# Both feed-forward products by one level of Strassen's algorithm, with the activations in DRAM

## The chip, the cores and the metric

The kernel runs on one core of a Trainium2 chip. A core has five engines that run side by side and meet only at semaphores: TensorE (matrix products, in the profile PE, with its weight loads as PEld), VectorE (DVE), ScalarE (ACT), GpSimd (POOL) and SyncE (SP), which here only issues DMAs. TensorE writes to PSUM, a small memory of eight banks of 128 x 512 float32; everything else works in SBUF. The metric is the device time of one execution in microseconds, lower is better, as the median of several runs.

## The reference

Four batches of eight heads of 768 tokens with 64 features each go through an attention in which a query sees only the keys of its own hash bucket, and then through a gated feed-forward block. Float64 weights come in, float32 goes out.

```python
q_bucket, k_bucket = 6-bit hashes of q @ proj > 0, k @ proj > 0     # proj is 64 x 6
mask = q_bucket[:, :, :, None] == k_bucket[:, :, None, :]
scores = where(mask, q @ k.T / 8, -1e9)
x = softmax(scores) @ v                     # (4, 8, 768, 64) -> 3072 tokens x 512
h = x @ w_in                                # 512 x 2048
g = h * (1.0 / (1.0 + exp(-1.702 * h)))
out = g @ w_out                             # 2048 x 512 -> 3072 x 512
```

## The kernel before

**Attention** (`attention`, from L198) works on 16 pairs: two heads of one batch at a time, side by side on the 128 partitions. A pair is cut into groups `(n, c, kt)`: a half `c` of its queries and two blocks of 128 keys, six groups a pair. For each key block `scores` (L268) writes the products of keys and queries for both heads to a PSUM tile `ps`: first the float32 product of `kT` and `qT`, then, added to it in the same PSUM tile, a bf16 product of the bit features `kf` and `qf`, which is zero where the buckets match and very large and negative where they don't. ScalarE takes the exponential of it into `es` (L276). One group later `values` (L294) multiplies `es` with `v` into `av`, and `add` (L280) adds the key blocks up, two of three additions on GpSimd (L286) and the rest on VectorE (L289, L292). At the end of a half, `total` (L302) sums over the partitions with a matmul (`dn`), `invert` (L308) makes the reciprocal on VectorE, and `norm` (L319) writes the result into `xT`, which holds all 3072 tokens as the right-hand operand of the feed-forward. During pair n, pair n + 1 is loaded, turned and hashed (`turn`, `hashed`, `featured`), and one chunk of 128 x 512 of `w_in` is converted from float64 bits to float32 (`convert`, L122): four VectorE passes, a square on ScalarE (L140), an addition on GpSimd (L144), and a last VectorE pass (L147) that waits for it.

After the last group, L388 to L391 find the largest squared norm, by a reduction, a transpose on TensorE and another reduction. Should it be too large, a safe form of everything (`shifted_attention` and a second feed-forward) runs after L525; with these inputs it doesn't.

**Feed-forward** (`feed_forward`, L465) goes over six blocks of 512 tokens. `hidden` (L492) makes the 2048 rows of `g` for one block: 16 PSUM tiles `h`, each the sum of four matmuls of 128 x 128 weights with 512 tokens, each followed by the activation on ScalarE (L499). `outputs` (L502) makes the 512 tokens' results: four PSUM tiles `y`, each the sum of 16 matmuls with 128 x 128 of `g` as weights and 512 columns of `w_out`, copied by VectorE (L510) and stored (L512). `g` stays in SBUF. While `hidden(0)` and `hidden(1)` run, `w_out` is converted, one chunk of 128 x 512 for every two activations.

**Order.** TensorE, VectorE, ScalarE and GpSimd run their instructions in the order in which the program writes them; the DMA issues on SP are placed by the framework. A tile pool gives every name a number of buffers; a new tile waits until the one that had its buffer before has been read for the last time. Pools are freed at the end of their `with` or `ExitStack`, and what comes after waits for the last readers of that memory.

Of the kernel before, what the change touches and what calls it, by code (L numbers as in the profile page):

```python
# [19 lines left out]
P = 128  # L20
# [18 lines left out]
def kernel(  # L39
# [57 lines left out]
    for x, signs in (("q", (1.0, -1.0)), ("k", (-1.0, 1.0))):  # L97
# [4 lines left out]
        for j in range(2):  # L102
# [11 lines left out]
    w_out_sb = const.tile([P, FC, DM], F32, name="w_out_sb")  # L114
# [5 lines left out]
    CW = 512  # L120

    def convert(cv, dst, src):  # L122

        raw = cv.tile([P, CW, 2], U32, tag="raw", name="raw")
        nc.sync.dma_start(out=raw, in_=src)
        lo, hi = raw[:, :, 0], raw[:, :, 1]
# [12 lines left out]

        nc.scalar.activation(size, hi.bitcast(F32), Act.Square)  # L140
        yield
        nc.vector.scalar_tensor_tensor(dst, lo, 2.0**-52, sign.bitcast(F32), op0=Alu.mult, op1=Alu.mult)  # L142
        yield
        nc.gpsimd.tensor_tensor(dst, bits.bitcast(F32), dst, op=Alu.add)  # L144
        yield

        nc.vector.scalar_tensor_tensor(dst, size, (1.125 * 2.0**-15) ** 2, dst, op0=Alu.is_ge, op1=Alu.mult)  # L147
# [3 lines left out]
    in_chunks = [(w_in_sb[:, kc, f : f + CW], wi[kc, :, f : f + CW]) for f in range(0, FF, CW) for kc in range(KC)]  # L151
    out_chunks = [(w_out_sb[:, fc, d : d + CW], wo[fc, :, d : d + CW]) for fc in range(FC) for d in range(0, DM, CW)]


    def load(ld, n, v_bufs=2):
# [39 lines left out]
        return steps  # L195


    def attention():  # L198


        actx = ExitStack()
        with actx:
            ld = actx.enter_context(tc.tile_pool(name="ld", bufs=1))
            wk = actx.enter_context(tc.tile_pool(name="wk", bufs=2))
            ep = actx.enter_context(tc.tile_pool(name="ep", bufs=1))
            cv = actx.enter_context(tc.tile_pool(name="cv", bufs=1))
            st = actx.enter_context(tc.tile_pool(name="st", bufs=2))
            sps = actx.enter_context(tc.tile_pool(name="sps", bufs=2, space=PSUM))
            aps = actx.enter_context(tc.tile_pool(name="aps", bufs=2, space=PSUM))
            mps = actx.enter_context(tc.tile_pool(name="mps", bufs=2, space=PSUM))  # L210


            es = [ep.tile([P, T, 2, HS + 1], F32, name=f"e{i}") for i in range(2)]
# [43 lines left out]
                                     start=True, stop=True)  # L257

            def featured(n, name):
                f = wk.tile([P, HS], BF16, tag=f"{name}b", name=f"{name}b")  # L260
                nc.vector.tensor_scalar(f, dots.pop((n, name)), above[name][:, 0:1], FEAT[name], op0=Alu.is_gt, op1=Alu.mult)
                for j in range(2):
                    for c in range(2):
                        r0 = D * c + 32 * j
                        nc.sync.dma_start(out=feats[n % 2][name][D * j : D * j + 32, c * HS : (c + 1) * HS],  # L265
                                          in_=f[r0 : r0 + 32, :])

            def scores(n, c, kt):  # L268
                qT, kT, qf, kf = xts[n, "q"], xts[n, "k"], feats[n % 2]["q"], feats[n % 2]["k"]
                keys, cols = slice(kt * P, (kt + 1) * P), slice(c * HS, (c + 1) * HS)  # L270
                ps = sps.tile([P, 2, 512], F32, tag="s", name="ps")
                for a, m, last in ((kT, qT, False), (kf, qf, True)):
                    for j in range(2):
                        hs = slice(D * j, D * (j + 1))
                        nc.tensor.matmul(ps[:, j, 0:HS], a[hs, keys], m[hs, cols], start=not last, stop=last)  # L275
                nc.scalar.activation(es[c][:, kt, :, 0:HS], ps[:, :, 0:HS], Act.Exp, scale=1.0 / D**0.5)  # L276
# [31 lines left out]
            def invert(n, c):  # L308
# [7 lines left out]
                rd = accs[n, c] = st.tile([P, HS], F32, tag="rd", name="rd", bufs=1)  # L316
                nc.vector.transpose(rd.rearrange("p (s i) -> p s i", i=32), r.to_broadcast([P, HS // 32, 32]))  # L317

            def norm(n, c):  # L319
# [11 lines left out]

            def step():
                next(conv[0], None)


            fetch(0, "k")
# [8 lines left out]
            for g in range(len(groups) + 3):  # L345
# [27 lines left out]
                if n < last:  # L373
# [11 lines left out]
            for _ in conv[0]:  # L385
                pass

            nc.vector.tensor_reduce(largest, sizes, axis=AX.X, op=Alu.max)  # L388
            row = mps.tile([1, P], F32, tag="m", name="row")
            nc.tensor.transpose(row, largest, ident)  # L390
            nc.vector.tensor_reduce(largest[0:1, 0:1], row, axis=AX.X, op=Alu.max)  # L391


    def shifted_attention():
# [67 lines left out]
                    nc.scalar.copy(xT[:, hp, s0 : s0 + HS], av)  # L462


    def feed_forward(tag, convs=()):  # L465
        NT = 512
        G = NT // P
        outv = out.rearrange("(b t p) d -> b t p d", b=B, p=P)
        with ExitStack() as fctx:
            gp = fctx.enter_context(tc.tile_pool(name=f"gp{tag}", bufs=2))  # L470
            op = fctx.enter_context(tc.tile_pool(name=f"op{tag}", bufs=3))
            fps = fctx.enter_context(tc.tile_pool(name=f"fps{tag}", bufs=4, space=PSUM))
            gs = {}

            def conversions():

                todo = [convert(cv, *x) for x in convs]
                for x in todo[:1]:
                    next(x)
                for i, x in enumerate(todo):  # L480
                    for y in todo[i + 1 : i + 2]:
# [6 lines left out]
            if convs:  # L488
                cv = fctx.enter_context(tc.tile_pool(name="cv2", bufs=2))
            steps = conversions()  # L490

            def hidden(n):  # L492
                g = gs[n] = gp.tile([P, FC, NT], F32, tag="g", name="g")
                for fc in range(FC):
                    h = fps.tile([P, NT], F32, tag="h", name="h")
                    for kc in range(KC):
                        nc.tensor.matmul(h, w_in_sb[:, kc, fc * P : (fc + 1) * P], xT[:, kc, n * NT : (n + 1) * NT],  # L497
                                         start=(kc == 0), stop=(kc == KC - 1))
                    nc.scalar.activation(g[:, fc, :], h, Act.Gelu_apprx_sigmoid)  # L499
                    next(steps, None)  # L500

            def outputs(n):  # L502
                g = gs.pop(n)
                for i in range(G):
                    y = fps.tile([P, DM], F32, tag="y", name="y")
                    for fc in range(FC):
                        nc.tensor.matmul(y, g[:, fc, i * P : (i + 1) * P], w_out_sb[:, fc, :],  # L507
                                         start=(fc == 0), stop=(fc == FC - 1))
                    o = op.tile([P, DM], F32, tag="o", name="o")
                    nc.vector.tensor_copy(o, y)  # L510
                    b, t = divmod(n * G + i, T)
                    nc.sync.dma_start(out=outv[b, t], in_=o)  # L512

            hidden(0)
            for n in range(N // NT):
                if n + 1 < N // NT:
                    hidden(n + 1)
                outputs(n)

    with tc.manual_schedule(engines=ORDERED):  # L520
        attention()
        feed_forward("", out_chunks)

    unsafe = nc.values_load(largest[0:1, 0:1].bitcast(I32)) >= SAFE_BITS
    with tc.If(unsafe):  # L525
        shifted_attention()
        feed_forward("2")


# [25 lines left out]
```

## Time and profile before

| | |
|---|---|
| median of 3 runs | 1047.54 us (1047.33 to 1049.24) |
| the profiled execution | 1048.01 us |
| its span, first to last instruction | 1046.1 us |
| mean granted TensorE clock | 0.995 of full speed |
| VectorE, ScalarE, GpSimd busy | 361.5, 255.7, 164.8 us |
| DMA | 45.81 MB, 44 GB/s over the span |

The profile is of one execution. Its rows give an engine, the source line, what the instruction writes and reads, how often it occurs, the busy time and the mean duration of one, and then how long the engine stood idle before these instructions and what it was waiting for. A float32 matmul is two TensorE instructions, each with a weight load of its own. The chain of work that ended last goes back from the last instruction to whatever released it, step by step, and so shows what the time consists of. A row of the windows view gives a stretch, its length, the busy time and number of instructions of PE, PEld, DVE, ACT and POOL, then the granted clock, the DMA engines' busy share and the GB/s that they moved. Timeline rows give the start, the duration, the engine and the instruction.

### The profile page before, as it was taken

How to read it: one execution, taken by the hardware profiler on the slowest of the kernel's cores; microseconds unless marked ns; L12 is line 12 of the kernel's file. 1: busy time of each engine (PE TensorE's matmuls, PEld its weight loads, DVE VectorE, ACT ScalarE, POOL GpSimd, SP SyncE). 2: the span in 40 equal slices, each digit the busy share in tenths (PEclk: the TensorE clock that was granted, in tenths of full speed). 3: DMA queues.
4: the chain of work that ended last, by engine and by line, in shares of the span. 5: the costliest groups of instructions: out<-in, count | busy, mean ns of one | idle time of the engine just before them, and what ended most of it. 6: DMA issues, size and time to landing. Idle time of an engine off the chain costs nothing.

```text
span 1046.1 us, 9494 instructions
## 1 busy us (share of the span) xinstructions
PE 1020.6 (98%) x3713; PEld 441.2 (42%) x3713; DVE 361.5 (35%) x578; ACT 255.7 (24%) x386; POOL 164.8 (16%) x108
## 2 busy tenths in 40 slices
PE   5999999999999979999999999999999999999997
PEld 2444444444444434444444444444444444444443
DVE  3787888878888754443000000000000000000000
ACT  3555555555555522222001100110011000110000
POOL 2343443344343411111000000000000000000000
PEclk9999999999999989999999999999999999999999
DMA  6444443444443012221000000000000000000000
GB/s 107 81 95 94 94 92 76 82 92 95 85 86 73 26 60 68 73 81 41 21 20 1 0 11 20 10 1 10 21 10 1 10 11 21 1 1 21 20 21 22
DMA packets 139862, 45.81 MB, mean 44 GB/s; under 512 B 128544, under 2 KB 132640, under 8 KB 139808
## 3 DMA queue, kind: packets, MB, share of 16 engines
q1 hardware_dynamic: 139808, 45.11, 18.6%
q8 instruction: 31, 0.51, 0.2%
q14 instruction: 23, 0.19, 0.1%
HBM read 35.65 MB, written 6.29 MB: 40 GB/s over the span
## 4 chain that ended last, share of the span: by engine, by line
PE 97%; DVE 1%; SPq 1%; DMA 0%; issue 0%; POOL 0%; DVEq 0%
PE h L497 32%; PE y L507 32%; PE ps L275 17%; PE av L299 13%; PE hash L256 2%; PE dn L306 2%; SPq L265 0%; SPq L233 0%; DMA k<-in_k_dram 0%; DVE w_in_sb L147 0%; DVE acc L292 0%; DMA qf<-qb 0%; POOL w_in_sb L144 0%; DVE rt L313 0%; DVE rd L317 0%
## 5 line engine op out<-in xcount | busy, mean ns | idle before, releaser
L497 PE MATMUL h<-xT,w_in_sb 128*128 128x512 f32 x768 | 332.5, 595 | 0.4 <-DVE largest L391 0.4
L507 PE MATMUL y<-w_out_sb,g 128*128 128x512 f32 x768 | 330.4, 592 | 0.0
L497 PEld LDWEIGHTS h<-xT,w_in_sb 128*128 128x128 f32 x768 | 146.6, 191 | 185.0 <-issue 184.3
L507 PEld LDWEIGHTS y<-w_out_sb,g 128*128 128x128 f32 x768 | 145.9, 190 | 183.7 <-issue 183.4
L510 DVE COPY o<-y 128x512 f32<-128x512 f32 x24 | 16.6, 693 | 531.4 <-PE y L507 531.4
L276 ACT ACTIVATE e<-ps 128x768 f32<-128x768 f32 x192 | 151.2, 813 | 173.3 <-PE ps L275 173.1
L499 ACT ACTIVATE g<-h 128x512 f32<-128x512 f32 x96 | 57.3, 597 | 478.8 <-PE h L497 478.8
L275 PE MATMUL ps<-qT,kT 64*128 64x384 f32 x768 | 167.6, 514 | 0.0
L286 POOL TENSOR_TENSOR acc<-e 128x768 f32<-128x768 f32 x64 | 121.3, 1904 | 166.6 <-ACT size L140 92.8
L299 PE MATMUL av<-e,v 128*64 128x385 f32 x768 | 145.2, 499 | 0.0
L275 PEld LDWEIGHTS ps<-qT,kT 64*128 64x128 f32 x768 | 64.0, 188 | 79.5 <-issue 50.0
L299 PEld LDWEIGHTS av<-e,v 128*64 128x64 f32 x768 | 46.7, 136 | 80.2 <-issue 72.9
L275 PE MATMUL ps<-qf,kf 64*128 64x384 bf16 x384 | 64.2, 324 | 3.5 <-DMA qf<-qb 3.5
L292 DVE TENSOR_TENSOR acc<-acc,acc 128x768 f32<-128x768 f32 x64 | 61.3, 958 | 5.6
L147 DVE SCALAR_TENSOR_TENSOR w_in_sb<-size,w_in_sb 128x512 f32<-128x512 f32 x16 | 32.3, 2016 | 10.6 <-POOL w_in_sb L144 10.6
L144 POOL TENSOR_TENSOR w_out_sb<-bits,w_out_sb 128x512 f32<-128x512 f32 x16 | 20.3, 1269 | 98.4 <-DVE w_out_sb L142 85.6
L138 DVE TENSOR_SCALAR sign<-bits 128x512 uint32<-128x512 uint32 x32 | 35.1, 1097 | 0.5
L275 PEld LDWEIGHTS <-kf 64*128 64x128 bf16 x384 | 19.7, 95 | 29.3 <-issue 5.0
L313 DVE STREAM_TRANSPOSE rt<-dn 128x384 f32<-128x384 f32 x32 | 18.7, 584 | 37.9 <-PE dn L306 37.9
L147 DVE SCALAR_TENSOR_TENSOR w_out_sb<-size,w_out_sb 128x512 f32<-128x512 f32 x16 | 11.1, 693 | 59.1 <-ACT size L140 59.1
L306 PE MATMUL dn<-acc,ones 128*64 128x384 f32 x128 | 26.1, 486 | 3.9 <-DVE acc L292 3.9
L289 DVE SCALAR_TENSOR_TENSOR acc<-e 128x768 f32<-128x768 f32 x32 | 29.9, 933 | 0.0
(57 smaller groups left out, 302.5 us busy)
## 6 DMA issues: line engine op xcount, KB each, us to landing
raw<-in_moe_w_in_dram SPq DMA_DIRECT2D x16, 512.0 KB, 3.5
raw<-in_moe_w_out_dram SPq DMA_DIRECT2D x16, 512.0 KB, 3.3
k<-in_k_dram SPq DMA_DIRECT2D x64, 96.0 KB, 3.1
q<-in_q_dram SPq DMA_DIRECT2D x64, 96.0 KB, 3.0
v<-in_v_dram SPq DMA_DIRECT2D x32, 192.0 KB, 3.1
out_dram<-o SPq DMA_DIRECT2D x24, 256.0 KB, 2.0
kf<-kb SPq DMA_DIRECT2D x64, 24.0 KB, 1.8
qf<-qb SPq DMA_DIRECT2D x64, 24.0 KB, 1.8
```

The lines of the kernel that those rows point to most:

```text
L138: nc.vector.tensor_scalar(sign, bits, 0xFF800000, None, op0=Alu.bitwise_and)
L147: nc.vector.scalar_tensor_tensor(dst, size, (1.125 * 2.0**-15) ** 2, dst, op0=Alu.is_ge, op1=Alu.mult)
L275: nc.tensor.matmul(ps[:, j, 0:HS], a[hs, keys], m[hs, cols], start=not last, stop=last)
L276: nc.scalar.activation(es[c][:, kt, :, 0:HS], ps[:, :, 0:HS], Act.Exp, scale=1.0 / D**0.5)
L286: nc.gpsimd.tensor_tensor(acc, e[:, kt - 1, :, 0:HS], e[:, kt, :, 0:HS], op=Alu.add)
L289: nc.vector.scalar_tensor_tensor(acc, e[:, 4, :, 0:HS], T * TINY, e[:, 5, :, 0:HS], op0=Alu.add, op1=Alu.add)
L292: nc.vector.tensor_tensor(acc, acc, accs.pop((n, c, o)), op=Alu.add)
L299: nc.tensor.matmul(av[D * j : D * (j + 1), :], vt[:, kt, j, :], es[c][:, kt, j, :], start=(kt == 0), stop=(kt == T - 1))
L306: nc.tensor.matmul(dn[D * j : D * (j + 1), :], ones, acc[:, j, :], start=True, stop=True)
L497: nc.tensor.matmul(h, w_in_sb[:, kc, fc * P : (fc + 1) * P], xT[:, kc, n * NT : (n + 1) * NT], start=(kc == 0), stop=(kc == KC - 1))
L499: nc.scalar.activation(g[:, fc, :], h, Act.Gelu_apprx_sigmoid)
L507: nc.tensor.matmul(y, g[:, fc, i * P : (i + 1) * P], w_out_sb[:, fc, :], start=(fc == 0), stop=(fc == FC - 1))
```

## The change

A product of two matrices, each cut into 2 x 2 quarters, needs eight products of quarters. Strassen's algorithm, here in Winograd's form, needs seven, with four sums of quarters on either side and seven additions of the results. Both feed-forward products are now made so.

For the weights `w_in`, for `x` (per block of 1024 tokens), for `g` (per block of 512) and for `w_out`, the sums overwrite one quarter and fill three new tiles. `in_sums` runs on GpSimd during pairs 9 and 10 (first half) and after the last pair (second half); the sums of the first 1024 tokens of `x` on VectorE in pairs 11 and 12.

The feed-forward is a generator of tasks. A task makes seven products, each in one PSUM bank, and combines them into four quarters of the result with one ScalarE copy and seven VectorE additions, each with a PSUM operand. Phase one (3 blocks of tokens x 8 = 24 tasks): a product is two matmuls of 128 x 128 weights with 512 tokens; the four results go through the activation and are stored to `g_dram`. Phase two (6 tasks of 512 tokens): a product is two times eight matmuls with 128 x 128 of `g` as weights and 256 columns of `w_out`; `g` comes back from DRAM, 4.19 MB for a task, into the memory that held `xT` and `w_in`. The sums for the next task run on VectorE in the midst of the present one. `w_out` is converted in tasks 1 to 16, one chunk each, and its sums run on GpSimd behind tasks 17 to 20.

The first task is issued right behind the last group's `values`, ahead of the last `total`, `invert` and `norm`; its PSUM banks are those of `ps`. From task 1 on, four more banks come from the pools of `av` and `dn`. The test for large norms (`guard`) moves into the last pair. `scores` makes the bit product first. `kb` and `qb` have one buffer each instead of two, and `rd` uses the memory of `rt`. The branch for large norms converts `w_in` again; it isn't taken.

```diff
-                for a, m, last in ((kT, qT, False), (kf, qf, True)):
+                for a, m, last in ((kf, qf, False), (kT, qT, True)):
...
+    def sums_a(eng, a11, a12, a21, a22, s1, s2, s4):
+        return [lambda: eng.tensor_tensor(s1, a21, a22, op=Alu.add),
+                lambda: eng.tensor_tensor(a21, a11, a21, op=Alu.subtract),
+                lambda: eng.tensor_tensor(s2, s1, a11, op=Alu.subtract),
+                lambda: eng.tensor_tensor(s4, a12, s2, op=Alu.subtract)]
+    def sums_b(eng, b11, b12, b21, b22, t1, t2, t4):
+        return [lambda: eng.tensor_tensor(t1, b12, b11, op=Alu.subtract),
+                lambda: eng.tensor_tensor(b12, b22, b12, op=Alu.subtract),
+                lambda: eng.tensor_tensor(t2, b22, t1, op=Alu.subtract),
+                lambda: eng.tensor_tensor(t4, b21, t2, op=Alu.subtract)]
...
+            extra = {HP * done + 1: in_sums(0) + sums_b(nc.vector, *quarters_x(0))}
...
+                if n == last and at == 1:
+                    guard()
...
+                    if at == 1:
+                        rest += extra.pop(n, [])
+                    if at in (2, 5) and rest:
+                        rest.pop(0)()
+                if g == len(groups):
+                    for _ in conv[0]:
+                        pass
+                    for f in in_sums(1):
+                        f()
+                    early.close()
+                    next(ff)
...
+            def task(mm, emit, mid=(), end=()):
+                u, v, c12, c21, c22 = (stage.tile([P, XT], F32, tag=x, name=x) for x in ("u", "v", "c12", "c21", "c22"))
+                def product(i):
+                    turn[0] += 1
+                    ps = sets[turn[0] // 4 % len(sets)].tile([P, XT], F32, tag="p", name="product")
+                    mm(i, ps)
+                    return ps
+                nc.scalar.copy(u, product(1))
+                nc.vector.tensor_tensor(v, product(6), u, op=Alu.add)
+                nc.vector.tensor_tensor(c21, product(7), v, op=Alu.add)
+                p = product(5)
+                nc.vector.tensor_tensor(c22, p, c21, op=Alu.add)
+                emit(1, 1, c22)
+                nc.vector.tensor_tensor(c12, p, v, op=Alu.add)
+                nc.vector.tensor_tensor(u, product(2), u, op=Alu.add)
+                emit(0, 0, u)
+                for x in mid:
+                    x()
+                nc.vector.tensor_tensor(c12, product(3), c12, op=Alu.add)
+                emit(0, 1, c12)
+                nc.vector.tensor_tensor(c21, product(4), c21, op=Alu.add)
+                emit(1, 0, c21)
+                for x in end:
+                    x()
+                if todo:
+                    todo.pop(0)()
...
+            LEFT = dict(zip(range(1, 8), (0, 1, 6, 3, 4, 5, 2)))
+            RIGHT = dict(zip(range(1, 8), (0, 2, 3, 6, 4, 5, 1)))
+            def hidden(sb, mt):
+                wq, xq = quarters_in(slice(mt * P, (mt + 1) * P)), quarters_x(sb)
+                def mm(i, ps):
+                    for kc in range(K2):
+                        nc.tensor.matmul(ps, wq[LEFT[i]][:, kc, :], xq[RIGHT[i]][:, kc, :],
+                                         start=(kc == 0), stop=(kc == K2 - 1))
+                def emit(i, j, c):
+                    nc.scalar.activation(c, c, Act.Gelu_apprx_sigmoid)
+                    t0 = (2 * sb + j) * XT
+                    nc.sync.dma_start(out=g_dram[i * (FC // 2) + mt, :, t0 : t0 + XT], in_=c)
+                steps = sums_b(nc.vector, *quarters_x(sb + 1)) if mt == FC // 2 - 1 and sb + 1 < n1 else []
+                return mm, emit, steps[:3], steps[3:]
...
+            def fetch(n):
+                for x, (i, k) in zip(g_views(n), ((0, 0), (0, 1), (1, 0), (1, 1))):
+                    t0 = n * XT + i * G2
+                    src = g_dram[k * (FC // 2) : (k + 1) * (FC // 2), :, t0 : t0 + G2].rearrange("c p t -> p c t")
+                    nc.sync.dma_start(out=x, in_=src)
...
+            def outputs(n):
+                gq = g_views(n)
+                def mm(i, ps):
+                    ps = ps.rearrange("p (m d) -> p m d", d=D2)
+                    for m in range(G2 // P):
+                        for c in range(FC // 2):
+                            at = LEFT[i]
+                            x = gq[at][:, c] if at < 4 else gq[at][:, c // (FC // 4), c % (FC // 4)]
+                            nc.tensor.matmul(ps[:, m, :], x[:, m * P : (m + 1) * P], wqs[RIGHT[i]][:, c, :],
+                                             start=(c == 0), stop=(c == FC // 2 - 1))
+                def emit(i, j, c):
+                    nc.sync.dma_start(out=outv[n, i, j], in_=c.rearrange("p (m d) -> p m d", d=D2))
+                return mm, emit
...
+            for sb in range(n1):
+                for mt in range(FC // 2):
+                    n = sb * (FC // 2) + mt
+                    if n == 1:
+                        sets.append(fctx.enter_context(tc.tile_pool(name=f"f1{tag}", bufs=4, space=PSUM)))
...
+                        todo += [lambda: (next(steps), next(steps))] * FC
+                        todo += sums_b(nc.gpsimd, *wqs)
+                    if (sb, mt) == (n1 - 1, 0):
+                        fetch(0)
+                    mm, emit, mid, end = hidden(sb, mt)
+                    if (sb, mt) == (n1 - 1, FC // 2 - 1):
+                        g0 = g_sums(0)
+                        mid, end = g0[:2], g0[2:]
+                    task(mm, emit, mid, end)
+                    yield
+            fetch(1)
+            for n in range(n2):
+                mm, emit = outputs(n)
+                task(mm, emit, g_sums(n + 1) if n + 1 < n2 else ())
+                if n + 2 < n2:
+                    fetch(n + 2)
+                yield
```

More of the change, by code (lines that the diff above doesn't have):

```diff
@@ L149 @@
     wi = w_in.bitcast(U32).rearrange("(kc ki) (f two) -> kc ki f two", ki=P, two=2)
     wo = w_out.bitcast(U32).rearrange("(fc fi) (d two) -> fc fi d two", fi=P, two=2)
[L151 to L152 removed]
+    in_chunks = [(w_in_sb[:, kc, f : f + CW], wi[kc, :, f : f + CW])
+                 for f0 in range(0, FF // 2, CW) for f in (f0, FF // 2 + f0) for kc in range(KC)]
@@ L195, in prepare, with attention @@
         return steps
-    def attention():
+    def attention(ff):
         actx = ExitStack()
@@ L333, in step, with guard @@
                 next(conv[0], None)
+            done = XT * 2 // S + (XT * 2 % S > 0)
+            extra = {HP * done + 1: in_sums(0) + sums_b(nc.vector, *quarters_x(0))}
+            rest = []
+            def guard():
+                nc.vector.tensor_reduce(largest, sizes, axis=AX.X, op=Alu.max)
+                row = mps.tile([1, P], F32, tag="m", name="row")
+                nc.tensor.transpose(row, largest, ident)
+                nc.vector.tensor_reduce(largest[0:1, 0:1], row, axis=AX.X, op=Alu.max)
             fetch(0, "k")
@@ L384, in attention @@
                         step()
[L385 to L391, printed above, removed]
+                    if at == 1:
[5 more added lines that the diff above has]
+                        pass
+                    assert not rest and not extra
+                    for f in in_sums(1):
+                        f()
+                    early.close()
+                    next(ff)
     def shifted_attention():
@@ L486, in conversions @@
                     yield
[L488 to L512, printed above, removed]
@@ L520, with whole @@
+            fetch(1)
[5 more added lines that the diff above has]
+                yield
+            assert not todo
+    def whole(steps):
+        for _ in steps:
+            pass
     with tc.manual_schedule(engines=ORDERED):
-        attention()
-        feed_forward("", out_chunks)
+        ff = feed_forward("")
+        attention(ff)
+        whole(ff)
@@ L524 @@
     unsafe = nc.values_load(largest[0:1, 0:1].bitcast(I32)) >= SAFE_BITS
     with tc.If(unsafe):
+        with tc.tile_pool(name="cv3", bufs=1) as cv:
+            for x in in_chunks:
+                whole(convert(cv, *x))
+        for f in in_sums(0) + in_sums(1):
+            f()
         shifted_attention()
-        feed_forward("2")
+        for f in sums_b(nc.vector, *quarters_x(0)):
+            f()
+        whole(feed_forward("2"))
 _INS = ["q", "k", "v", "proj", "moe_w_in", "moe_w_out"]
```

83 lines of the change are left out of this document (56 added, 27 removed).

## The prediction

> **What bounds the kernel now.** I read the busy table and the chain of work that ended last, then the costliest groups, then the chain in order of time for where the stages begin and end, and last the stretches (windows) for clock and DMA.
>
> ```profile
> PE 1020.6 (98%) x3713; PEld 441.2 (42%) x3713; DVE 361.5 (35%) x578; ACT 255.7 (24%) x386; POOL 164.8 (16%) x108
> PE 97%; DVE 1%; SPq 1%; DMA 0%; issue 0%; POOL 0%; DVEq 0%
> L497 PE MATMUL h<-xT,w_in_sb 128*128 128x512 f32 x768 | 332.5, 595 | 0.4 <-DVE largest L391 0.4
> L507 PE MATMUL y<-w_out_sb,g 128*128 128x512 f32 x768 | 330.4, 592 | 0.0
> L507 PEld LDWEIGHTS y<-w_out_sb,g 128*128 128x128 f32 x768 | 145.9, 190 | 183.7 <-issue 183.4
> ```
> ```profile
> 378.92 112.07 PE h L497 x256
> 490.99 54.93 PE y L507 x128
> ...
> 930.46 109.88 PE y L507 x256
> ```
>
> TensorE is the bound from end to end: 97% of the chain is its work. The feed-forward (FF) runs without a hole from 378.92 to 1040.34 us. One float32 matmul of 512 columns is two instructions (384 matmuls, 768 rows), each 54.93/128 = 0.4291 us; the listed mean of 595 ns counts overlapping ends and is not used. The weight load takes 190 ns and lies beneath. So the time falls by whatever TensorE instructions go away, if nothing new makes it wait.
>
> **The multiplications.** Phase one has 24 tasks of 7 products of 2 matmuls: 672 instructions of 512 columns for 768, 96 x 0.4291 = **41.2 us saved**. Phase two has 6 tasks of 7 products of 16 matmuls: 1344 instructions, but of 256 columns. No matmul of that length with a full 128x128 float32 load stands in the trace. If all of 0.4291 scales, one is 0.2146. While the clock was cold the loads, one per matmul, followed each other thus:
>
> ```profile
> 379.94 0.34 PEld L497 LDWEIGHTS h<-xT,w_in_sb 128*128 128x128 f32 x1 [0.52 <-issue]
> 380.79 0.34 PEld L497 LDWEIGHTS h<-xT,w_in_sb 128*128 128x128 f32 x1 [0.52 <-issue]
> 381.64 0.34 PEld L497 LDWEIGHTS h<-xT,w_in_sb 128*128 128x128 f32 x1 [0.52 <-issue]
> 382.50 0.34 PEld L497 LDWEIGHTS h<-xT,w_in_sb 128*128 128x128 f32 x1 [0.52 <-issue]
> ```
>
> That is 0.853 each at what the windows below show as about half clock; half of it is 0.4267, so some 2.5 ns of the warm 0.4291 is fixed, and I take 0.2133 + 0.0025 = 0.2158. 1344 x 0.2158 = 290.0 against 768 x 0.4291 = 329.6: **39.5 us saved**, provided that a 190 ns load still hides beneath 216 ns. The nearest evidence is in the attention, where a short bf16 matmul stands ahead of a float32 load:
>
> ```profile
> 359.17 0.92 PE L275 MATMUL ps<-qT,kT 64*128 64x384 f32 x4
> 359.92 0.33 PE L275 MATMUL ps<-qf,kf 64*128 64x384 bf16 x2
> 360.08 0.81 PE L275 MATMUL ps<-qT,kT 64*128 64x384 f32 x4
> 360.73 0.33 PE L275 MATMUL ps<-qf,kf 64*128 64x384 bf16 x2
> 360.99 1.51 PE L299 MATMUL av<-e,v 128*64 128x385 f32 x8
> ```
> ```profile
> 359.92 0.36 PEld L275 LDWEIGHTS ps<-qT,kT 64*128 64x128 f32 x4 [0.22 <-issue]
> ```
>
> The load begins with the bf16 pair at 359.92 and the float32 matmul follows 0.16 us later, though one such load lasts about 0.19. A matmul thus need not wait for the whole of its load, and 160 ns of cover was enough; 216 should be. The bounds are 0.2146 below and, above, 0.1 us exposed per instruction, which is what the same rows show where nothing covers the load: the first float32 block, behind av, takes 0.75, the second 0.65.
>
> The Trainium skill, TensorE: Matmul & The Clock Gate, section Back-to-back issue gap, speaks against short matmuls: in a stream of loads and matmuls both set the spacing, about 81 ns at N=128 where a matmul alone takes 56. Here the 160 ns case argues for full cover; charging those 25 ns to each 256-column instruction would, as an estimate, add 34 us and give 997.
>
> **The seam.**
>
> ```profile
> 368.15 2.81 PE L299 MATMUL av<-e,v 128*64 128x385 f32 x16
> 374.87 0.87 PE L306 MATMUL dn<-acc,ones 128*64 128x384 f32 x4 [3.90 <-DVE acc L292]
> 377.32 0.62 DVE L325 SCALAR_TENSOR_TENSOR xT<-av,vs,rd 128x384 f32<-128x384 f32 x1
> 378.18 0.37 PE L390 MATMUL row<-ident,largest 128*1 128x128 f32 x1 [2.44 <-DVE largest L388]
> ```
> ```profile
> 18.00:371.00 353.00, 352.91 (x2160) 147.19 (x2158) 281.53 (x404) 185.01 (x268) 140.61 (x80) 1.00 0.40 82
> 371.00:379.00 8.00, 1.32 (x6) 0.36 (x6) 6.10 (x11) 0.00 (x0) 0.34 (x1) 0.81 0.00 0
> 379.00:383.30 4.30, 4.30 (x6) 1.96 (x7) 1.94 (x5) 0.00 (x0) 0.00 (x0) 0.55 0.64 244
> ```
>
> From the last av (370.96) to 378.92 TensorE does 1.24 us in 7.96: 6.7 idle, then half clock, which costs 112.07 - 2 x 54.93 = 2.2. Task 0 now stands right behind the last av, in front of dn, and its activations are two batches old: **8.9 us saved**. Three things come back. First, guard() moves into pair 15, behind this chain:
>
> ```profile
> 355.17 0.81 PE L306 MATMUL dn<-acc,ones 128*64 128x384 f32 x4
> 356.91 0.58 DVE L317 STREAM_TRANSPOSE rd<-r 128x384 f32<-128x384 f32 x1
> ```
>
> dn ends at 355.98, VectorE leaves the chain at 357.49 and reduces 0.18; TensorE, which now goes on with scores, stands at the transpose in between: 1.8 us. Second, in_sums(1) runs on GpSimd beside the last three additions:
>
> ```profile
> L286 POOL TENSOR_TENSOR acc<-e 128x768 f32<-128x768 f32 x64 | 121.3, 1904 | 166.6 <-ACT size L140 92.8 <-DVE acc L292 50.7 <-ACT e L276 23.0
> L292 DVE TENSOR_TENSOR acc<-acc,acc 128x768 f32<-128x768 f32 x64 | 61.3, 958 | 5.6
> L147 DVE SCALAR_TENSOR_TENSOR w_in_sb<-size,w_in_sb 128x512 f32<-128x512 f32 x16 | 32.3, 2016 | 10.6 <-POOL w_in_sb L144 10.6
> L147 DVE SCALAR_TENSOR_TENSOR w_out_sb<-size,w_out_sb 128x512 f32<-128x512 f32 x16 | 11.1, 693 | 59.1 <-ACT size L140 59.1
> ```
>
> L147 takes 693 ns alone and 2016 with L286 beside it: VectorE is held for the GpSimd instruction. The Trainium skill, SBUF — State Buffer, section SBUF: two separate sides, calls this an exclusive lock held for a whole instruction; the rows agree. GpSimd adds 1904/768 = 2.48 ns an element, so its four additions of 1024 take 2.54 us each. If each of three VectorE additions is held once (7.6 us), task 0's first PSUM reads slip by 3.5 us past the point where its sixth product needs a bank, since only four banks are free then. Bounds 0 and 3.5; I take 1.8. Third, task 1's first product uses a bank of the pools of av and dn, whose last reader comes 2.2 us behind dn (375.74 to 377.94): 0 to 2.2, I take 1.2. **4.8 us back.**
>
> **What must stay hidden.** Phase one: a task lasts 28 x 0.4291 = 12.0 us.
>
> ```profile
> L510 DVE COPY o<-y 128x512 f32<-128x512 f32 x24 | 16.6, 693 | 531.4 <-PE y L507 531.4
> L325 DVE SCALAR_TENSOR_TENSOR xT<-av,vs,rd 128x384 f32<-128x384 f32 x32 | 19.8, 618 | 1.1
> L499 ACT ACTIVATE g<-h 128x512 f32<-128x512 f32 x96 | 57.3, 597 | 478.8 <-PE h L497 478.8
> L144 POOL TENSOR_TENSOR w_out_sb<-bits,w_out_sb 128x512 f32<-128x512 f32 x16 | 20.3, 1269 | 98.4 <-DVE w_out_sb L142 85.6
> ```
>
> VectorE adds seven times from PSUM at 0.69 (L510) to 0.75 (L325's 618 ns plus 128 elements): about 5.0 us. In tasks 1 to 16 it also converts one chunk, and waits at L147 behind L144 (1.27):
>
> ```profile
> 383.30:491.00 107.70, 107.70 (x252) 47.67 (x252) 48.32 (x91) 28.19 (x47) 20.30 (x16) 1.00 0.21 69
> ```
>
> The 48.32 us cover some 15 chunks, 3.2 each; with the wait 4.7, together under 10 of 12.0. At the two changes of token block four additions of 1024 are added (958 ns + 256 x 1.04 = 1.22 each, 4.9): 15 of 12 once, and with eight banks TensorE may run eight products, 13.7 us, ahead. ScalarE needs five passes and a square, under 4 us. Without this cover each microsecond over 12.0 would cost 16 us. In the attention the eight extra additions fall into pairs 9 to 12, where VectorE is 281.53/353 = 80% busy: nothing. GpSimd's four w_out sums (2048 elements, 5.1 us each) fall into tasks 17 to 20, where conversions have ended.
>
> Phase two: a task lasts 48.3 us, a product 6.9. VectorE does 5 us of evacuation and four sums of 2048 elements, 2.28 each. Fetches are 4.19 MB a task, queued on SP behind the previous task's outputs, so issued about as a task begins, and needed when the sums start after five products, 34.5 us on. The windows give 82 GB/s at DMA share 0.40, so 205 at full use with mostly tiny packets: 20 us. Sums then end by 44, and product 6 of the next task first reads s2 at 55. Hidden. Phase one's 1.05 MB of writes per 12.0 us plus a 0.5 MB raw chunk is 131 GB/s. The SP waits that these issues add stand in front of later stores alone, each with a second buffer one task away.
>
> **The order of the bit products** exchanges blocks but leaves two changes of array shape per group (to and from av), where the exposed 0.1 us stands: nothing, with bounds of 0.1 us x 96 groups = 9.6 both ways. Single buffers for kb and reuse of rt are rewritten a pair or three groups later: nothing.
>
> **Sum.** 41.2 + 39.5 + 8.9 - 4.8 = 84.8. Span 1046.1 - 84.8 = 961.3. The profiled execution took 1048.01, 1.9 more than its span, so 963.2; it lies 0.5 above the median, so **963**. The drain behind the last matmul (1040.34 to 1046.1) stays: one VectorE pass and one store.
>
> **Rivals.** (a) Loads partly show in phase two. For: eight av instructions take 1.44, less the 0.1 exposed 0.335 a pair, against 385/512 x 0.4291 = 0.323, so a stream can lose 12 ns. Against: L497 loses none. 1344 x 12 ns = 16 us: 979. (The rule of the Trainium skill above names the same mechanism at a higher price.) (b) **Slower**: each 256-column instruction exposes the whole 0.1 us, as at a change of shape. 134 us: 1097. It decides from 84.8/1344 = 63 ns upward. Against it stands the 160 ns case. (c) Fetches move no faster than the attention's mean of 82 GB/s: 51 us, sums to 58 where s2 is wanted at 55, five times 3 us: 978. Against: the cold window moved 244. (d) The change doesn't do what it says: VectorE, not TensorE, paces phase one, at say 15 us a task for 16 tasks, 48 us: 1011. For: 10 of 12 is near; against: every price in it is a row.
>
> **Chances.** Forecast (950 to 972) 0.68, (a) 0.13, (b) 0.05, (c) 0.05, (d) 0.09. The bounds kept are -3.0 (seam), -1.6 (0.2146), -9.6 (order) below: 949; above +3 (seam), +9.6 (order) and (a)'s 16: 991. A measurement of this kernel tells about 0.2% (2 us) from no change. Faster 0.94, same 0.01, slower 0.05.
>
> **What would show it.** Phase two's matmuls: 1344 at 0.216 us each, six stretches of 48 us; 0.23 is (a), above 0.28 is (b). Phase one: 24 stretches of 12.0. TensorE idle on VectorE in tasks 1 to 16 is (d); VectorE idle on fetches is (c). No idle stretch at 371, clock 1.00 there, and 1 to 2 us idle in pair 15. The attention's groups still 3.26 us. I am wrong if the 256-column spacing isn't half.

## The result, and the profile after

The changed kernel takes 960.91 us (median of 4 runs, 960.23 to 961.26) beside 1048.39 us (1047.33 to 1050.23) for the kernel before on the same chip (the three runs of the table further up and one more): a ratio of 0.916, with a 95% interval from 0.915 to 0.918. The forecast was 963. The profiled execution has a span of 959.2 us at a mean clock of 0.996.

The busy table and the chain's shares by engine, from the page of the changed kernel:

```profile
PE 931.4 (97%) x4193; PEld 528.4 (55%) x4193; DVE 563.2 (59%) x800; ACT 275.3 (29%) x416; POOL 204.7 (21%) x120
PE 90%; DVE 6%; DMA 2%; SPq 1%; issue 1%; POOL 0%; DVEq 0%
```

TensorE is still busy for 97% of a span that is 87 us shorter. The weight loads went from 42% to 55%, VectorE from 35% to 59%: the work that replaced the eighth product lies beside TensorE. The chain now leaves TensorE for 10% of the time, where it left it for 3%; most of that isn't idle time of TensorE, which is busy for 931.4 of 959.2 us.

The chain in order of time, changed kernel (start, duration, what):

```profile
364.83 2.74 PE av L339 x16
367.58 12.37 PE product L571 x28
379.94 0.82 PE dn L346 x4
...
382.32 0.63 DVE xT L365
...
383.09 278.32 PE product L571 x644
661.40 290.09 PE product L613 x1344
```

The first product follows the last av without a hole. Phase two is 1344 instructions in 290.09 us, 0.2158 each. Stretches of the changed kernel (PE, PEld, DVE, ACT, POOL busy, clock, DMA share, GB/s): pairs 9 to 12, the end of the attention, the start of task 1, a task of phase one with a conversion, one with the change of token block, two tasks of phase two and what follows the last matmul:

```profile
216.00:310.00 94.00, 92.42 (x580) 37.73 (x576) 85.94 (x116) 49.65 (x73) 49.62 (x26) 1.00 0.44 87
348.00:367.60 19.60, 17.97 (x114) 7.38 (x110) 11.80 (x23) 8.68 (x11) 7.73 (x5) 1.00 0.01 1
383.10:390.00 6.90, 6.90 (x12) 2.92 (x13) 0.69 (x1) 0.59 (x1) 0.00 (x0) 0.75 0.00 0
```
```profile
395.70:407.70 12.00, 12.00 (x30) 5.30 (x29) 7.85 (x14) 3.56 (x6) 1.26 (x1) 1.00 0.38 132
467.90:479.90 12.00, 12.00 (x29) 5.32 (x28) 10.34 (x16) 2.91 (x5) 1.27 (x1) 1.00 0.30 109
```
```profile
709.70:758.10 48.40, 48.40 (x226) 42.61 (x225) 13.64 (x11) 0.59 (x1) 0.00 (x0) 1.00 0.34 109
903.10:951.50 48.40, 48.38 (x225) 42.25 (x223) 4.75 (x7) 0.59 (x1) 0.00 (x0) 1.00 0.07 23
```
```profile
951.50:959.20 7.70, 0.00 (x0) 0.00 (x0) 0.69 (x1) 0.00 (x0) 0.00 (x0) 0.67 0.13 42
```

Read from the top: 1.6 us idle in pairs 9 to 12; 1.6 idle in pair 15; a cold start of task 1; then every task of phase one is 12.0 us without a hole, VectorE busy for 7.9 of 12 us with a conversion and for 10.3 at a change of token block, and every task of phase two 48.3 to 48.4. Behind the last matmul stand 7.7 us, where 5.8 stood before.

Where the 86.9 us of span came from: the attention's last av ends 3.4 us earlier (370.96 to 367.58), from parts of either sign that the experiments take apart; what lies between it and the feed-forward's unbroken run fell from 7.96 to 3.15 (379.94 to 383.09, now behind task 0), 4.8; phase one from 329.6 + 2.2 (its cold start) to 290.7, 41.1; phase two from 329.6 to 290.1, 39.5; and 1.9 is given back at the end.

### The profile page after: what moved, and what is told of

Same layout as the page of the kernel before. It is cut to its first block, busy times and chain, and to the rows that moved or that the text cites. A ratio compares the mean times of both kernels' runs of the same rounds, so it can differ in the third digit from the quotient of the medians.

```text
span 959.2 us, 11272 instructions
## 1 busy us (share of the span) xinstructions
PE 931.4 (97%) x4193; PEld 528.4 (55%) x4193; DVE 563.2 (59%) x800; ACT 275.3 (29%) x416; POOL 204.7 (21%) x120
## 4 chain that ended last, share of the span: by engine, by line
PE 90%; DVE 6%; DMA 2%; SPq 1%; issue 1%; POOL 0%; DVEq 0%
PE product L571 30%; PE product L613 30%; PE ps L315 14%; PE av L339 12%; PE dn L346 2%; PE hash L296 2%; DVE acc L332 1%; DMA raw<-in_moe_w_in_dram 1%; DVE acc L329 1%; DVE sign L147 1%; DVE kT L284 0%; DVE rt L353 0%; DVE rt L357 0%; SPq L305 0%; SPq L273 0%
## 5 line engine op out<-in xcount | busy, mean ns | idle before, releaser
L571 PE MATMUL product<-xT,w_in_sb 128*128 128x512 f32 x288 | 136.4, 596 | 2.3 <-DVE xT L365 2.3
L575 ACT ACTIVATE c<-c 128x512 f32<-128x512 f32 x72 | 45.3, 631 | 182.4 <-DVE c L546 132.4
L571 PEld LDWEIGHTS product<-xT,w_in_sb 128*128 128x128 f32 x288 | 54.7, 190 | 71.5 <-issue 65.1
L571 PE MATMUL product<-t_x,s_in 128*128 128x512 f32 x192 | 91.1, 597 | 0.0
L613 PE MATMUL product<-t_out,xT 128*128 128x256 f32 x288 | 63.6, 379 | 0.0
L613 PE MATMUL product<-w_out_sb,xT 128*128 128x256 f32 x288 | 63.6, 379 | 0.0
L613 PE MATMUL product<-w_out_sb,w_in_sb 128*128 128x256 f32 x288 | 63.6, 379 | 0.0
L571 PEld LDWEIGHTS product<-t_x,s_in 128*128 128x128 f32 x192 | 36.9, 192 | 47.0 <-issue 47.0
L613 PEld LDWEIGHTS product<-w_out_sb,xT 128*128 128x128 f32 x288 | 54.7, 190 | 7.9 <-issue 0.5
L613 PEld LDWEIGHTS product<-t_out,xT 128*128 128x128 f32 x288 | 54.7, 190 | 7.4
```

Source lines behind the costliest of these rows:

```text
L571: nc.tensor.matmul(ps, wq[LEFT[i]][:, kc, :], xq[RIGHT[i]][:, kc, :], start=(kc == 0), stop=(kc == K2 - 1))
L575: nc.scalar.activation(c, c, Act.Gelu_apprx_sigmoid)
L613: nc.tensor.matmul(ps[:, m, :], x[:, m * P : (m + 1) * P], wqs[RIGHT[i]][:, c, :], start=(c == 0), stop=(c == FC // 2 - 1))
```

## The experiments

Unless another kernel is named, "more" and "less" below are against the 960.91 us of the changed kernel. The kernel before, run beside each set of experiments, had medians from 1048.39 to 1049.63 us, so about 1 us of such a difference can come from the occasion rather than from the edit.

**The order of the products alone.** In the changed kernel, a group's two score blocks take 1.72 us of the chain where they took 1.82, so the prediction's "nothing" for the order was in doubt. Two kernels make the edit alone, one in each direction.

```diff
-                for a, m, last in ((kT, qT, False), (kf, qf, True)):
+                for a, m, last in ((kf, qf, False), (kT, qT, True)):
```

> The kernel before with nothing changed but the order in scores: bit product first. If the order itself shortens a group of the attention from 3.26 to 3.17 us, as the changed kernel's trace shows, 96 groups give 9 us back, and the first group loses about 1 us because TensorE now waits for the first bit features before anything else: 1040 us. Rival: the shorter groups of the changed kernel come from something else in it (where its tiles lie), and the order is worth nothing, as the prediction had it: 1048 us, groups of 3.26.

> The changed kernel with the old order in scores. If the order is worth 9.6 less 1.2 us: 969 us, groups of 3.26, and the feed-forward as it was (583 us from the first product to the last). Rival (order worth nothing): 961 us.

Measured: 1041.91 us beside 1049.63 for the kernel before (ratio 0.993, 0.991 to 0.995), and 968.24 for the changed kernel with the old order, 7.3 more than with the new. The chains, first of the kernel before with the new order, then of the changed kernel with the old:

```profile
306.37 1.72 PE ps L275 x12
308.09 1.44 PE av L299 x8
```
```profile
363.30 1.82 PE ps L315 x12
365.12 1.44 PE av L339 x8
```

The 0.1 us goes with the order and with nothing else: 96 x 0.1 = 9.6, less what the first group loses. That loss can be seen where the attention starts (the first scores, and the DMA that TensorE waits for in the chain), in the kernel before and in the changed one:

```profile
18.21 4.13 PE ps L275 x19
22.34 1.45 PE av L299 x8
```
```profile
14.89 2.62 DMA qf<-qb
17.51 0.14 issue
17.64 5.83 PE ps L315 x24
23.47 1.45 PE av L339 x8
```

With the scores first, five of 24 instructions are done before the bit features land and av starts at 22.34; with the bit product first, all 24 come after and av starts at 23.47: 1.1 us (1.4 and 0.5 in the two pairs of kernels that differ in the order alone). The net of 8.5 is near the 7.3 and 7.7 measured. In the changed kernel the shorter groups also leave VectorE less time before dn needs its sum. TensorE's waits for that, in the changed kernel and then with the old order:

```profile
PE dn L346 <- DVE acc L332: 1.6, 4, 0.5
```
```profile
PE dn L346 <- DVE acc L332: 0.6, 2, 0.4
```

That is 1.0 us (total, times, longest), most of what the 7.3 lacks.

What becomes shorter is shown by the timeline of the changed kernel, TensorE alone:

```profile
271.26 0.34 PE L315 MATMUL ps<-qf,kf 64*128 64x384 bf16 x2
271.43 0.81 PE L315 MATMUL ps<-qT,kT 64*128 64x384 f32 x4
272.08 0.33 PE L315 MATMUL ps<-qf,kf 64*128 64x384 bf16 x2
272.24 0.81 PE L315 MATMUL ps<-qT,kT 64*128 64x384 f32 x4
272.98 1.51 PE L339 MATMUL av<-e,v 128*64 128x385 f32 x8
```

Behind av, the bf16 block takes 0.17 us and the second one 0.16; in the old order the float32 block behind av took 0.75 and the second 0.65. So the 0.1 us that stood at the change of array shape is gone on that side; on the other side (the last scores end at 272.24 + 0.65 = 272.89, av starts at 272.98) it stays.

**The banks of task 1.** The 2.3 us at 380.76 to 383.09 and the cold clock behind them were put down to the first product's bank.

```diff
-                    if n == 1:
+                    if n == 2:
                         sets.append(...)
+                    if n == 1:
                         wop = ...
```

> The changed kernel with the second four PSUM banks taken at task 2 instead of task 1, so that task 1's first product doesn't wait for the last reader of av. If that wait is the cause of the 2.3 us idle at 380.7 and of the stretch at 0.75 clock behind it (1.9 us more), 4 us go: 957 us. Rival: task 1, on four banks alone, waits for VectorE's evacuation instead: 960 to 961 us, with idle or held matmuls inside task 1.

Measured: 958.30 us (957.99 to 958.96), 2.6 less. The chain of this kernel:

```profile
368.32 12.36 PE product L571 x28
380.69 0.80 PE dn L346 x4
381.48 276.58 PE product L571 x644
```

Both the idle time (3.15 us between dn's start and the next product, now 0.80) and the cold stretch (278.32 us, now 276.58) are gone, the way from the first product to phase two is 4.1 us shorter, and four banks carry task 1. That the bank caused the wait is shown; that the cold stretch belongs to the wait is likely, but the kernel with the late guard below has the wait without it. The total gained less than 4.1, as this execution's attention ended 0.7 us later (368.32 for 367.58) and its end was 0.4 longer.

**How near phase two is to its weight loads.** The forecast stood on a 190 ns load hiding beneath 216 ns.

```diff
+                        for d in range(0, D2, P):
                             for c in range(FC // 2):
-                            nc.tensor.matmul(ps[:, m, :], x[...], wqs[RIGHT[i]][:, c, :], ...)
+                                nc.tensor.matmul(ps[:, m, d : d + P], x[...], wqs[RIGHT[i]][:, c, d : d + P], ...)
```

> The changed kernel with every phase-two matmul of 256 columns made as two of 128, each with its own weight load: 2688 instructions. A: loads hide but cannot follow each other faster than the 190 ns that one takes; the matmul alone would take 0.109, so the spacing is 0.190, phase two takes 511 us instead of 290 and the kernel about 1182 us. B: only half a load (95 ns) stands in the way of the next: spacing 0.109, phase two 294, the kernel 965 us. C: load and matmul do not overlap at this length: spacing 0.30, phase two 804, the kernel 1475 us.

Measured: 971.68 us (one run), 10.8 more. Phase two of this kernel, as the windows view gives it, its row of the chain, and the row of a group of its loads:

```profile
662.30:962.30 300.00, 300.00 (x2688) 299.88 (x2686) 79.69 (x66) 4.74 (x8) 0.00 (x0) 1.00 0.27 87
```
```profile
662.22 300.17 PE product L614 x2688
```
```profile
L614 PEld LDWEIGHTS product<-w_out_sb,xT 128*128 128x128 f32 x576 | 65.1, 192 | 0.5 <-issue 0.5
```

2688 instructions take 300.2 us in the chain, 0.1117 each, although a load is listed at 192 ns. That is B, with 3.8 ns on top of half of 0.2158. Loads follow one another faster than one lasts, so their listed duration is not the distance that they need, and at 256 columns phase two is not near a limit that they set. A and C fall.

**The guard.**

```diff
-                nc.vector.tensor_reduce(largest, sizes, axis=AX.X, op=Alu.max)     # in guard()
...
                 if n == last and at == 1:
+                    nc.vector.tensor_reduce(largest, sizes, axis=AX.X, op=Alu.max)
+                if n == last and at == 3:
                     guard()
```

> The changed kernel with guard's transpose and second reduction two groups later than its first reduction. If TensorE's 1.6 us idle in pair 15 is the wait for VectorE's chain (dn, two transposes, reduction), it goes: 959.3 us, the transpose itself (0.3) stays. Rival: TensorE meets another wait at once, since VectorE is behind anyway: 961 us.

Measured: 958.30 us (957.76 to 958.45), 2.6 less. The 1.6 us are gone (57 of 57 us busy from 310 to 367); the profiled execution also shows 276.62 us for the 644 products, so no cold stretch, although TensorE waits the same 2.3 us ahead of them:

```profile
378.77 0.82 PE dn L346 x4
381.91 276.62 PE product L572 x644
```

The wait that the guard caused is gone, as expected; the other 1 us of the gain would fit the missing cold stretch, which isn't shown to be the edit's doing.

**The sums of pairs 9 to 12.** Four waits of dn on acc, 0.3 to 0.5 us each, stand in pairs 9 to 12 of the changed kernel, each behind a sum at a pair's end. In pairs 11 and 12 that sum is VectorE's own. In pairs 9 and 10 it is GpSimd's, and VectorE's addition beside it lasts 2.2 us where it takes 0.95 alone; for pair 9, GpSimd's row and VectorE's in the chain:

```profile
235.46 2.81 POOL L166 TENSOR_TENSOR w_in_sb<-w_in_sb 128x1024 f32<-128x1024 f32 x1
```
```profile
236.94 2.16 DVE acc L329
```

So two of the four waits are the hold that the prediction priced at the seam alone.

```diff
-                    if at in (2, 5) and rest:
+                    if (at == 2 or n == last and at == 5) and rest:
```

> The changed kernel with the eight sums of pairs 9 to 12 spread, one a pair at its third group (the last at the end of pair 15). If the sums at a pair's end hold the additions that dn waits for, as the four waits of dn on acc in pairs 9 to 12 suggest, these four waits go and with them 1.6 to 2.4 us: 958.5 to 959.3 us. Rival: those pairs lose their time to the sums as such, wherever they stand: 961 us, with the waits in other pairs.

Measured: 963.04 us (961.85 to 964.27), 2.1 more: a miss. The four waits are gone, and TensorE is busy throughout 216 to 310:

```profile
216.00:310.00 94.00, 94.00 (x594) 38.98 (x594) 85.06 (x116) 50.72 (x74) 48.63 (x26) 1.00 0.44 88
```

A new wait took their place. VectorE at the end of the attention in this kernel, and then TensorE, from the timeline:

```profile
365.65 1.21 DVE L176 TENSOR_TENSOR t_x<-xT,t_x 128x1024 f32<-128x1024 f32 x1
366.78 3.10 DVE L329 SCALAR_TENSOR_TENSOR acc<-e 128x768 f32<-128x768 f32 x1
369.92 6.00 DVE L332 TENSOR_TENSOR acc<-acc,acc 128x768 f32<-128x768 f32 x2
375.84 0.68 DVE L543 TENSOR_TENSOR v<-product,u 128x512 f32<-128x512 f32 x1
```
```profile
371.60 1.88 PE L571 MATMUL product<-xT,w_in_sb 128*128 128x512 f32 x4
376.67 3.75 PE L571 MATMUL product<-xT,s_in 128*128 128x512 f32 x4 [3.19 <-DVE v L543]
```

The eighth sum, placed at the very end, lets GpSimd's in_sums(1) start before the last three additions; each is held for one GpSimd instruction (3.0 to 3.1 us for 0.95). Task 0 meets its sixth product without a bank, waits 3.2 us and goes on at a lower clock (3.75 us for four instructions that take 1.88 elsewhere). This is the hold that the prediction priced at 3.5 us; in the changed kernel it struck two additions and cost 0.4.

**The branch.** This kernel leaves out the safe form of the computation and the read of the norm that chooses it.

```diff
-    unsafe = nc.values_load(largest[0:1, 0:1].bitcast(I32)) >= SAFE_BITS
-    with tc.If(unsafe):
-        ...
```

> The changed kernel without the branch for large norms and without the read of the norm that decides on it (which leaves the safe form out). The span runs on for 7.7 us after the last matmul, 5.8 before the change. If the larger branch is the cause, at least 1.9 us go: 959 us or less, and the rest behind the last matmul is at most 5.8. Rival: the last store (1 KB rows instead of 2 KB) is the cause: 961 us and 7.7.

Measured: 957.98 us (957.77 to 959.40), 2.9 less. Its last matmul ends at 661.67 + 290.09 = 951.76 and the span at 956.0: 4.2 us for 7.7.

```profile
661.67 290.09 PE product L613 x1344
```

The branch and the read of the norm together cost 3.5 us behind the last matmul and not only the difference of 1.9; what in them costs it isn't shown, since no instruction of the branch is. The rival falls, as the last store is unchanged. That the larger branch makes the difference from 5.8 to 7.7 fits, but no run has the kernel before without its branch.

**All mended, twice.** The late banks, the late transpose, the spread sums, and the scores first in the first group alone:

```diff
-                for a, m, last in ((kf, qf, False), (kT, qT, True)):
+                order = [(kf, qf), (kT, qT)]
+                if n == c == 0 and kt < 2:
+                    order.reverse()
+                for i, (a, m) in enumerate(order):
```

> The changed kernel with the second four banks at task 2, the late transpose, the spread sums, and the scores first in the first group alone (so that TensorE doesn't wait for the first bit features). The parts as measured or read from the trace: 2.6 for the banks, 1.6 for the transpose, 1.6 to 2.4 for the sums, 1.1 for the first group: 953 to 954 us. If they stand in each other's shadow: 956 to 958.

Measured: 958.72 us where 953 to 954 was expected, and from 955.29 to 959.20 in five runs, the widest of all kernels here: the 3.2 us wait in task 0 is in it too. So the eighth sum went to pair 13:

```diff
-                    if (at == 2 or n == last and at == 5) and rest:
+                    if (at == 2 or n == 13 and at == 3) and rest:
```

> The last kernel (all four mends) with the eighth sum in pair 13 instead of at the end of pair 15. If that sum, standing ahead of the last additions on VectorE, is what let GpSimd's sums hold all three of them and cost 3.2 us idle in task 0 and a cold stretch in some executions, both go: 950.3 us of span, 952 us. Rival: the hold comes from in_sums(1) alone and stays: 955 to 959 us.

Measured: **953.14 us** (952.54 to 954.01), a ratio of 0.908 (0.907 to 0.910) to the kernel before. Once the first bit features have landed, TensorE waits only once up to its last product, for 0.3 us, and the wait in task 0 is gone: the eighth sum was its cause. The hold itself stays on the last two additions (the first row below). Last, in_sums(1) went behind the GpSimd part of the first two w_out chunks:

```diff
-                    for f in in_sums(1):
-                        f()
...
+                        for i, f in enumerate(() if tag else in_sums(1)):
+                            todo[i // 2] = lambda x=todo[i // 2], f=f: (x(), f())
```

> The kernel before in this list, with in_sums(1) two tasks later, behind GpSimd's part of the first two w_out chunks, so that nothing on GpSimd stands beside the last additions. If the hold is GpSimd's instruction and nothing else, L332 falls from 3 us to 1 us there, task 0 from 12.4 to 12.0 us: 952 us or 0.4 below the other. Rival (the additions are slow for another reason): they stay at 3 us.

Measured: 953.11 us, the same. VectorE's additions from 364 to 382 us, with in_sums(1) beside them and then without:

```profile
L335 DVE TENSOR_TENSOR acc<-acc,acc 128x768 f32<-128x768 f32 x2 | 5.9, 2952 | 0.1
```
```profile
L335 DVE TENSOR_TENSOR acc<-acc,acc 128x768 f32<-128x768 f32 x2 | 1.9, 958 | 0.1
```

2952 ns to 958: without GpSimd's sums beside them the additions take what they take elsewhere, so the rival falls. Task 0 goes from 12.36 to 12.21 us only, not to 12.0, too little for the median to tell.

**How much cover phase one has.**

```diff
-                        todo += [lambda: (next(steps), next(steps))] * FC
+                        todo += [lambda: [next(steps) for _ in range(4)]] * (FC // 2)
```

> The changed kernel with two chunks of w_out converted per task in tasks 1 to 8 instead of one in tasks 1 to 16. VectorE then has 4.8 us of additions, two conversions of 4.7 and some 3.5 us of waiting for the second chunk's load, 17.7 us in a task of 12.0. If VectorE's time counts as soon as it passes 12.0, less the 13.7 us that TensorE may run ahead, 8 x 5.7 - 13.7 = 32 us are lost: 993 us, with TensorE idle on VectorE from about task 3. Rival: the reserve of eight banks carries it: 961 us.

Measured: 993.76 us (one run). Stretches of 12 us of this kernel, from the first idle one on:

```profile
419.00:431.00 12.00, 11.44 (x27) 4.86 (x26) 9.29 (x17) 4.18 (x7) 1.26 (x1) 1.00 0.35 120
431.00:443.00 12.00, 9.07 (x21) 3.63 (x20) 7.41 (x14) 1.75 (x3) 2.52 (x2) 1.00 0.35 108
...
479.00:491.00 12.00, 3.21 (x8) 1.14 (x6) 8.16 (x13) 2.40 (x4) 1.73 (x2) 0.83 0.32 109
```

The reserve of banks lasts for some three tasks and then TensorE waits, though VectorE is nowhere busy for more than 9.4 of 12 us. VectorE stands in its own order: in each task it waits twice 1.4 us for GpSimd's part of a conversion and about 1.5 for the second chunk to land. What TensorE waited for (total, times, longest):

```profile
PE product L571 <- DVE v L543: 12.3, 5, 5.8
PE product L571 <- DVE t_x L175: 11.4, 1, 11.4
```

The agreement with 993 is luck in good part. From one task to the next VectorE takes 15.3 to 15.6 us and not the 17.7 of the working. The 11.4 us are a single wait for the sums of the next token block, which stand behind the conversions and were not in the working, and some 8 us are a low clock behind the waits (0.83 in the last row).

## Why the prediction was right, point by point

- **The multiplications.** Phase one was to take 288.4 us and takes 290.7, the 2.3 being task 0's hold and task 1's cold start. Phase two was to take 290.0 and takes 290.09. Splitting 0.4291 us into a part that scales and 2.5 ns that don't, from the cold rows, paid: 0.2158 came out to the digit. Rivals (a) and (b) fall by that figure, and the 128-column run shows that the loads still leave room. The surcharge of 25 ns (an estimate, 81 less 56 at 128 columns) that the Trainium skill's page TensorE: Matmul & The Clock Gate (section Back-to-back issue gap) would put on a short matmul is not there: 3.8 ns at 128 columns.
- **The seam.** Task 0 follows the last av without a gap and at full clock, as forecast; what came back behind task 0 is counted with the banks. Guard: 1.8 priced, 1.6 idle. The hold: right in mechanism, 0.4 against 1.8 taken, and 3.2 against the bound of 3.5 where it struck in full, with a cold stretch on top that the bound left out. The exclusive lock of the Trainium skill's page SBUF — State Buffer (section SBUF: two separate sides) agrees with 2952 against 958 ns.
- **The banks** were mis-sized: 1.2 taken, bound 2.2; measured 2.3 of idle and 1.7 of cold clock behind it, 4.1 in all. The bound had left out that a cold stretch can follow an idle one, though the seam of the kernel before had been priced with one.
- **What must stay hidden** stayed hidden in the feed-forward: 12.0 us a task in phase one, no wait for a fetch in phase two. Rivals (c) and (d) fall. In the attention "80% busy: nothing" was wrong by 1.6 us: VectorE's mean share says nothing of the four moments when dn waits for its last addition, and the hold by GpSimd's sums had been priced at the seam only.
- **The order** was the step that failed: "nothing, with bounds of 0.1 us x 96 groups". It argued that both changes of shape remain and each keeps its 0.1 us. They remain, but the first block behind av, if it is bf16, takes only 0.01 us longer than the second, where a float32 block took 0.1. Measured 7.3 to 7.7 us; the bound was right, the value at the wrong end, and the forecast's sign of groups of 3.26 us failed (3.17).
- **The drain** was to stay and grew by 1.9 us. The branch and the read of the norm are 3.5 of its 7.7 us.

In sum the 7 to 8 us that the order gained unforecast, and 1.4 too much set aside for the hold, were met by some 3 us of banks, 2 of the end and up to 1.6 in pairs 9 to 12; the rest, 1 us or so, isn't traced. That 963 stands so near 961 is partly luck, though the 81 us of the multiplications are not.

## What to carry to other kernels

Fewer multiplications pay in full where the additions that replace them lie beside TensorE; count an in-order engine's waits with its work, since at two chunks a task VectorE paced the kernel while it was busy for at most 9.4 us of 12. When work is moved away from a wait, look at what it now stands beside: the sums left four waits of up to half a microsecond and, spread out, made one of 3.2. And where two products go to the same bank, try both orders: it is one line, and here worth 0.7% with nothing else changed.

## What the runs showed of the hardware

- A wait of TensorE of the same length was followed by a low clock in some executions and not in others. With the 2.3 us ahead of task 1 the next 644 instructions took 278.32 us in the changed kernel, 278.32 with the old order and 278.19 without the branch, but 276.62 with the late guard. The 3.2 us in task 0 gave a cold stretch with spread sums and none in the profiled execution of the first mended kernel, which has the late guard too. In the cold ones TensorE had also stood idle for 1.6 us at the guard, some 25 to 30 us earlier; whether that matters is not shown, as each kernel was profiled once. The first mended kernel's spread of 4 us between runs would fit cold stretches in its other runs.
- Weight loads listed at 192 ns each followed one another every 112 ns.
- At a change of array shape the first block behind av took about 0.1 us longer than the next when it was float32 (0.75 and 0.65), and about 0.01 when it was bf16 (0.17 and 0.16). That this is an exposed weight load is a reading of the rows; why the two differ is not shown.
